# Two attention blocks mixed by a gate: the output projection is begun ahead of the second group of score products, which are issued inside it

## The chip, the cores and the metric

The kernel runs on one core of a Trainium2 chip. The metric is the device time of one execution in microseconds. PE is the matrix engine (PEld is its weight load), DVE the vector engine, ACT the scalar engine, POOL the GpSimd engine, SP the engine that issues most transfers.

## The reference

One input `x` (2048 x 512) goes through two attention blocks of 32 heads with 16 columns each, and a sigmoid gate mixes the results. Block A cuts the sequence into four segments, attends causally inside a segment and adds what a linear memory of the earlier segments gives. Block B is plain softmax attention over all 2048 positions.

```
g = sigmoid((x * gate_w).sum(-1))
# block A, segment s of 512 rows, per head
p = softmax(qs @ ks.T * 0.25 + causal mask)
o = sig(beta) * (phi(qs) @ M / (phi(qs) @ z)) + (1 - sig(beta)) * (p @ vs)
M, z = M + phi(ks).T @ vs, z + phi(ks).sum()
a = o_all @ A_wo
# block B, per head
b = softmax(q @ k.T * 0.25) @ v @ B_wo
out = g * a + (1 - g) * b
```

## The kernel before, in words

The first part projects `x` into q, k and v of both blocks, and the memory of block A is carried along. The order of the whole program is written out by hand; no planner reorders it. Only PSUM banks are picked while the program is being built, by rule: `bank(allowed)` takes the bank of the list that was used longest ago.

The second part is a loop `for k in range(32)`. Iteration `k` handles one unit of block A (four heads, one segment of 512 queries) and one of block B (four heads, the same 512 queries, all 2048 keys). It is cut into `NG` = 37 groups `n`: 32 of block B, 5 of block A. Each group does four things, and the rows of the profile carry their lines:

- `t_group` (L537): two score products with K, transposed (keys on partitions), `j` = 0 on rows 0 to 63 of the array and `j` = 1 on rows 64 to 127, each into a bank of its own out of the three banks `T3` = `tb0`, `tb1`, `mb`. Then two exponentials by ACT (L543) empty these banks into the tile `raw`.
- between the two products, one task of the row maxima for the next iteration, `s_b` (L474): two products on the two halves of the rows into one of two double banks, `sbk0` and `sbk1` (`rot("s", SBK)` alternates between them), and one DVE reduction over both (L476). In the text these are "the maxima products" and "the maxima reduction".
- `pv` (L559): four products of the exponentials of an earlier group with V into the bank `pvb`, on four column strips of the array.
- at set groups, side work. At group 0, the last `pv` of the previous unit of block A, and `fin_copy` (L566), a DVE copy of `pvb` to `pvs`.

From `k` = 9 to `k` = 30, group 1 also has `out_rows` (L644), one half of the output projection of a tile of 128 rows: twelve pairs of products on the two row halves, `j` = 0 into a bank from `misc()` (the oldest of `T3`), `j` = 1 into half of an `sbk`. Its left operands are `oh` and `ol`, the rounded part and the rest of the attention output, which `out_split` (L622 on ACT, L623 on POOL) makes at the end of each even iteration; the last four pairs use `ol`. After the third pair it runs the functions of its argument `inner`. The results leave by ACT (L652 or L658) and DVE (L653 or L659), in turn for `a` = 0 and `a` = 1. So the projection stands 22 times in the program, in eleven odd and eleven even iterations, the odd ones right behind an `out_split`.

Of the kernel before, what the change touches and what calls it, by code (L numbers as in the profile page):

```python
# [23 lines left out]
NT = SEQ // 128  # L24
# [10 lines left out]
def gated_mix_kernel(ctx, tc, xt, wq, wk, wv, wo, beta, wqkv, wob, gate_w, out):  # L35
# [49 lines left out]
    SBK = [PS.tile([128, 2, C], FT, name=f"sbk{i}") for i in range(2)]  # L85
    lru = []

    def bank(allowed):
        b = min(allowed, key=lambda a: max([n for n, x in enumerate(lru) if x is a], default=-1))
        lru[:] = [x for x in lru if x is not b] + [b]  # L90
        return b
# [3 lines left out]
    def misc():  # L95
        return bank(mode["misc"])
# [12 lines left out]
    def rot(key, lst):  # L109
        i = cnt.get(key, 0)  # L110
        cnt[key] = i + 1
        return lst[i % len(lst)]
# [287 lines left out]
    def q_of(u):  # L400
        return QA[u % 2] if u < 32 else QB[u % 3]

    def k_of(u, p):
        return KA[u % 2][:, p] if u < 32 else KB[(u - 32) % 3][:, p]

    def load_q(u):
        kd, qd, c = UN[u]
        load_qk(q_of(u), kd, 0, qd, c)

    def load_ka(u):  # L410
        kd, qd, c = UN[u]
        load_qk(KA[u % 2], kd, 1, qd, c)
# [105 lines left out]
    AT = {}  # L518
# [3 lines left out]
    def t_group(u, n, banks, between=()):  # L522


        kd, qd, c = UN[u]
        bs = [bank(banks) for _ in range(2)]
        c0 = 0
        for it, hs in (((n // 2, (n % 2 * 2, n % 2 * 2 + 1)),) if kd == "B" else GA[n]):
            q0 = 128 * it if kd == "A" else 0
            w = C - q0  # L530
            pn = it if kd == "B" else it % 2
            for j, h in enumerate(hs):
                if j:
                    for f in between:
                        f()
                r = slice(64 * j, 64 * j + 64)
                nc.tensor.matmul(bs[j][:, c0:c0 + w], k_of(u, h // 2)[r, 128 * it:128 * it + 128],  # L537
                                 q_of(u)[r, h // 2, q0:], start=True, stop=True)
                PT[u, it, h] = PTILE[pn % 2][:, 2 + j if (kd, it) == ("A", 2) else h][:, c0:c0 + w]
            c0 += w  # L540
        for j in range(2):
            pt = PTILE[pn % 2][:, 2 + j if (kd, n) == ("A", 4) else hs[j]]
            nc.scalar.activation(pt, bs[j], AF.Exp, scale=SCALE)  # L543
            if kd == "A":
                m = pt[:, :128] if n < 2 else pt.rearrange("p (a t) -> p a t", a=4)[:, ::3 if n < 4 else 2]
                nc.gpsimd.affine_select(out=m, in_=m, pattern=[[1, 128]] if n < 2 else [[0, 2], [1, 128]],  # L546
                                        compare_op=OP.is_ge, fill=0.0, base=0, channel_multiplier=-1)
# [89 lines left out]
            nc.sync.dma_start(outr[tt * 128:(tt + 1) * 128, :], AT["yo"])  # L637

    def out_rows(c, t, a, inner):
        b = [misc(), rot("s", SBK)[:, 0]]  # L640
        for n, (oi, wi, g) in enumerate([(oi, wi, g) for oi, wi in TERMS for g in range(4)]):
            for j in range(2):
                r = slice(64 * j, 64 * j + 64)
                nc.tensor.matmul(b[j], (AT["oh"], AT["ol"])[oi][r, g, a], (AT["wh"], AT["wl"])[wi][r, g, a],  # L644
                                 start=n == 0, stop=n == 11)
            if n == 2:
                for f in inner:
                    f()
                rot("s", SBK)
        if a == 0:  # L650
            AT["y"] = [AT["L"].tile([128, DM], FT, name=n) for n in ("yo", "yp")]
            nc.scalar.activation(AT["y"][0], b[0], AF.Copy)  # L652
            nc.vector.tensor_copy(AT["y"][1], b[1])  # L653
        else:
            tt = 4 * c + t
            y0, y1 = AT["y"]
            y2 = AT["L"].tile([128, DM], FT, name="yq")
            nc.scalar.activation(y2, b[0], AF.Copy)  # L658
            nc.vector.tensor_tensor(y1, b[1], y1, op=OP.add)  # L659
            nc.gpsimd.tensor_tensor(y0, y0, y2, op=OP.add)  # L660
            nc.gpsimd.tensor_tensor(y0, y0, y1, op=OP.add)
            nc.sync.dma_start(outr[tt * 128:(tt + 1) * 128, :], y0)
# [33 lines left out]
    def todo(fn, *a):  # L696
        return lambda: fn(*a)
# [90 lines left out]
    for blk in range(16):  # L788
# [9 lines left out]
        n = blk + 1 + (c == 2)  # L798
# [87 lines left out]
    T3 = TB + [MB]  # L886
# [4 lines left out]
    def pvs(k, n):  # L891

        ua, ub = k, 32 + k
        if n == 0:
            if k:
                pv(ua - 1, 2)
                fin_copy(ua - 1)
        elif k == 31 and n < 2 * NT:
            if n % 2 and n > 1:
                pv(ub, n // 2 - 1)  # L900
        elif 2 <= n < 2 * NT + 2:
            pv(ub, n // 2 - 1, n % 2 * 256, n % 2 * 256 + 256)
            if n == 2 * NT + 1:
                fin_copy(ub)
        elif n > 2 * NT + 1:
            m = n - 2 * NT - 2
            if m < 2:
                pv(ua, 0, 256 * m, 256 * m + 256)
            else:
                pv(ua, 1)  # L910
                pv(ua, 3)

    def extras(k):

        pre, post = {}, {}
        if not k:
            for n in range(4):
                pre[2 * n] = [fill[n - 4]]
        post[2 * S_LAST + 4] = [todo(m_rows, k + 1)]
        for n, at in [(k - 9, 1)] + [(23, 2 * OMI)] * (k == 31):  # L920
            if n >= 0:
                rows = (n // 8, n // 2 % 4, n % 2)
                pre[at] = [todo(out_rows, *rows, plan.pop((k, at))) if k < 31 else todo(out_mm, *rows)]
        return pre, post

    def beside(k, it):

        for f, it0, u in ((fin_load, NT + 1, 32 + k), (fin_rec, 5, 31 + k), (fin_bc, 6, 31 + k),
                          (fin_load, 1, k - 1), (fin_rec, 6, k - 1), (fin_bc, S_LAST + 2, k - 1)):
            if it == it0 and (k or it0 > NT):  # L930
                f(u)
        c, j = divmod(k - 1, 8)
        if k and j % 2:
            for kd, it0 in (("B", 9), ("A", 13)):
                if it == it0:
                    fin_norm(kd, j // 2, c)
        if k >= 8 and k % 2 == 0 and it == NT + 2:
            out_split(k // 8 - 1, k // 2 % 4)
        if (k, it) == (31, 4):
            grest = AT["grest"] = AT["o"][0][64:, 0, 0]  # L940
            nc.sync.dma_start(grest, GD[3 * C:].rearrange("(o t) -> o t", o=1).to_broadcast([64, C]))
        if (k, it) == (31, 9):
            grest = AT["grest"]
            nc.vector.tensor_scalar(grest, grest, nh[64:, 3:4], None, op0=OP.mult)
        if (k, it) == (31, NT + 2):
            fin_rec(63)
        if k == 31 and it == 13:
            o = AT["o"][1][:64, 3, 0]
            nc.gpsimd.tensor_tensor(o, o, AT["d"][0][:64], op=OP.mult)
        if k == 31 and it < 8 and it % 2 == 0:  # L950
            for a in range(2):
                tail_split(it // 2, slice(0, 3), a)


    plan = {}
# [14 lines left out]
    ex = [extras(k) for k in range(32)]  # L970
    for k in range(32):
        ua, ub = k, 32 + k
        banks = T3 + [b[:, 0] for b in SBK] * (k == 31)
        for n in range(NG):
            it = n // 2 if n < NG - 1 else NT + 2
            mid = plan.pop((k, n)) if n < 2 * NT and (k, n) in plan else []
            t_group(*(ub, n) if n < 2 * NT else (ua, n - 2 * NT), banks, mid)
            for f in plan.get((k, n), []) + ex[k][0].get(n, []):
                f()
            pvs(k, n)  # L980
            for f in ex[k][1].get(n, []):
                f()
            if n % 2 == 0 and n < NG - 1:
                continue
            beside(k, it)
            if it == S_LAST:
                m_chain(k + 1)
            if it == 4 and not k:
                late()
            if it == 4 and not k:  # L990
                load_q(ub + 2)
                for c in range(NC4):
                    load_kb(2, c)
            if it == NT and k < 29:
                load_q(ub + 3)
                load_kb(k + 3)
            if it == 6 and k < 31:
                load_q(ua + 1)
                load_ka(ua + 1)
                if (ua + 1) % 2 == 0:  # L1000
                    load_va(ua + 1)
            if it == 9:
                if k % 2 == 0 and k < 30:
                    load_vb(k // 2 + 1)
                if 1 <= k <= 4:
                    load_wo(k - 1)
# [55 lines left out]
```

## Time and profile before

| | |
|---|---|
| time, median of 3 runs | 1941.73 us (1938.82 to 1942.05) |
| profiled execution | 1942.89 us |
| its span in the trace | 1941.2 us |
| mean granted PE clock | 0.998 |
| busy share of the span | PE 99%, DVE 84%, ACT 74%, POOL 18% |
| first `out_rows` at | 787.71 us |

The profiled execution has its own time; the trace's span is 1.7 us shorter. The times within the trace are counted from the span's start. A busy PE counts a product from its start until a modelled end, so short stalls of PE are better read from start to start, or from the idle time of PEld.

### The profile page before, as it was taken

What the parts mean: (1) busy time and instruction counts of PE and PEld (TensorE: products, weight loads), DVE (VectorE), ACT (ScalarE), POOL (GpSimd) and SP (SyncE); (2) the same over time, 40 slices, a digit from 0 to 9 for tenths busy, and PEclk for the clock granted to TensorE, in tenths of its full rate; (3) what the DMA queues carried; (4) which work ended last, traced back from release to release, by engine and by line L of the source; (5) the groups of instructions that cost most, each with busy time, mean ns of one, the idle gap of its engine ahead of it and who ended that gap; (6) DMA issues with size and microseconds to landing.
All of it is one profiled execution on the core that took longest, in us unless ns stands there. A gap on an engine that the chain in (4) does not pass through costs nothing.

```text
span 1941.2 us, 44264 instructions
## 1 busy us (share of the span) xinstructions
PE 1915.3 (99%) x17749; PEld 933.8 (48%) x17749; DVE 1622.4 (84%) x1689; ACT 1438.0 (74%) x2710; POOL 345.1 (18%) x687
## 2 busy tenths in 40 slices
PE   7999998999999999999999999999999999999999
PEld 5887776444444444444444444444444444444445
DVE  6135765799999999999999999999999999999942
ACT  4233332688888888888888888888888888888894
POOL 5200000011211111112121212121212121212122
PEclk9999999999999999999999999999999999999999
DMA  7666556655543444444434344444444444434111
GB/s 218 167 208 189 183 186 180 162 118 115 100 116 88 106 90 105 88 115 86 115 88 115 88 115 88 109 95 109 95 101 99 95 104 92 107 90 107 50 49 59
DMA packets 163794, 222.54 MB, mean 115 GB/s; under 512 B 39916, under 2 KB 90556, under 8 KB 157828
## 3 DMA queue, kind: packets, MB, share of 16 engines
q1 hardware_dynamic: 159284, 211.41, 44.0%
q0 software_dynamic: 3248, 8.03, 2.2%
q8 instruction: 140, 2.29, 0.5%
q14 instruction: 66, 0.54, 0.1%
q10 hardware_dynamic: 1056, 0.26, 0.1%
HBM read 147.95 MB, written 68.16 MB: 111 GB/s over the span
## 4 chain that ended last, share of the span: by engine, by line
PE 95%; DVE 2%; DMA 1%; SPq 1%; ACT 0%; issue 0%; DVEq 0%; ACTq 0%
PE pvb L559 34%; PE tb L537 18%; PE sbk L474 12%; PE mb L537 9%; PE tb L304 4%; PE sbk L452 3%; PE tb L644 2%; PE mb L304 2%; PE sbk L287 1%; PE tb L287 1%; PE sbk L456 1%; PE mb L644 1%; PE pvb L304 1%; PE mb L287 1%; PE pvb L287 1%; DMA dA<-st 1%
## 5 line engine op out<-in xcount | busy, mean ns | idle before, releaser
L476 DVE TENSOR_REDUCE mxb<-sbk 128x2 f32<-128x1024 f32 x1024 | 1228.7, 1221 | 52.1 <-PE tb L537 24.0
L543 ACT ACTIVATE raw<-tb 128x512 f32<-128x512 f32 x1555 | 887.1, 598 | 125.7 <-PE tb L537 82.2
L559 PE MATMUL pvb<-raw,vb 128*17 128x256 f32 (+1 forms) x8072 | 639.8, 388 | 0.0
L543 ACT ACTIVATE raw<-mb 128x512 f32<-128x512 f32 x782 | 467.8, 598 | 60.3 <-PE mb L537 34.0
L474 PE MATMUL sbk<-xh,qb 64*128 64x512 f32 x1344 | 473.3, 442 | 4.8 <-DMA xh<-dB 3.4
L537 PE MATMUL tb<-qb,xh 64*128 64x512 f32 x872 | 351.2, 444 | 0.0
L559 PEld LDWEIGHTS pvb<-raw,vb 128*17 128x17 f32 x8072 | 134.9, 95 | 338.8 <-issue 333.4
L474 PE MATMUL sbk<-kb,qb 64*128 64x512 f32 x704 | 239.0, 442 | 0.0
L537 PEld LDWEIGHTS tb<-qb,xh 64*128 64x128 f32 x872 | 146.0, 184 | 174.4 <-issue 86.6
L537 PE MATMUL mb<-qb,xh 64*128 64x512 f32 x445 | 198.1, 445 | 0.0
L474 PEld LDWEIGHTS sbk<-xh,qb 64*128 64x128 f32 x1344 | 191.9, 184 | 11.6 <-DVE mxb L476 5.6
L537 PE MATMUL tb<-qb,kb 64*128 64x512 f32 x470 | 189.9, 444 | 0.8 <-DVE st L314 0.8
L546 POOL TENSOR_SCALAR_AFFINE_SELECT raw<-raw 128x256 f32<-128x256 f32 (+1 forms) x320 | 115.5, 361 | 354.2 <-ACT raw L543 346.3
L460 DVE TENSOR_REDUCE mx<-sbk 128x2 f32<-128x768 f32 (+1 forms) x128 | 136.7, 1090 | 23.2 <-POOL o L608 13.7
L537 PEld LDWEIGHTS mb<-qb,xh 64*128 64x128 f32 x445 | 82.0, 184 | 92.7 <-issue 47.9
L537 PEld LDWEIGHTS tb<-qb,kb 64*128 64x128 f32 x470 | 79.7, 184 | 96.1 <-issue 49.8
L537 PE MATMUL mb<-qb,kb 64*128 64x512 f32 x234 | 104.8, 448 | 0.0
L474 PEld LDWEIGHTS sbk<-kb,qb 64*128 64x128 f32 x704 | 96.7, 184 | 5.8 <-issue 3.2
L559 PE MATMUL pvb<-raw,va 128*17 128x256 f32 (+2 forms) x1280 | 94.8, 384 | 0.8 <-ACT pvs L568 0.8
L452 PE MATMUL sbk<-ka,qa 64*128 64x256 f32 (+3 forms) x512 | 87.8, 358 | 1.1
L311 ACT ACTIVATE st<-tb 128x512 fp32r<-128x512 f32 x33 | 19.8, 599 | 81.9 <-DVE phi L310 46.2
L603 POOL TENSOR_TENSOR o<-o,d 128x512 f32<-128x512 f32 x31 | 39.7, 1281 | 227.2 <-DMA d<-rd 177.1
(315 smaller groups left out, 2036.6 us busy)
## 6 DMA issues: line engine op xcount, KB each, us to landing
xh<-dB SPq DMA_DIRECT2D x38, 512.0 KB
vb<-vdB SPq DMA_DIRECT2D x16, 1088.0 KB
dB<-st SPq DMA_DIRECT2D x64, 256.0 KB
dA<-st SPq DMA_DIRECT2D x64, 256.0 KB
pd<-pvs SPq DMA_DIRECT2D x64, 256.0 KB
kb<-dB SPq DMA_DIRECT2D x22, 512.0 KB
xh<-dB SPq DMA_DIRECT2D x38, 256.0 KB
qb<-dB SPq DMA_DIRECT2D x64, 128.0 KB
```

Of the source, the lines that this page charges most:

```text
L287: nc.tensor.matmul(b, lhs, WV[wi][:, k, :], start=n == 0, stop=n == 11)
L304: nc.tensor.matmul(b, WS[ws][w][wi][:, k, :], (XH, XL)[xi][c][:, k, :], start=n == 0, stop=n == 11)
L452: nc.tensor.matmul(b[:, j, c0:c0 + n], q_of(u)[r, p, i * 128:(i + 1) * 128], k_of(u, p)[r, :n], start=True, stop=False)
L460: nc.vector.tensor_reduce(m[:, :, p, i], b[:, :, :n], axis=AX.X, op=OP.max)
L474: nc.tensor.matmul(b[:, j], q_of(u)[r, p, i * 128:(i + 1) * 128], k_of(u, p)[r, kc * C:(kc + 1) * C], start=True, stop=True)
L476: nc.vector.tensor_reduce(MXB[u][:, :, p, i, kc], b, axis=AX.X, op=OP.max)
L537: nc.tensor.matmul(bs[j][:, c0:c0 + w], k_of(u, h // 2)[r, 128 * it:128 * it + 128], q_of(u)[r, h // 2, q0:], start=True, stop=True)
L543: nc.scalar.activation(pt, bs[j], AF.Exp, scale=SCALE)
L546: nc.gpsimd.affine_select(out=m, in_=m, pattern=[[1, 128]] if n < 2 else [[0, 2], [1, 128]], compare_op=OP.is_ge, fill=0.0, base=0, channe ...
L559: nc.tensor.matmul(PVB[32 * h:32 * h + E + 1, q0 + lo:q0 + hi], vt[:, it, 4 * q + h, :], pt[:, lo:hi], start=it == 0 and lo == 0, stop=it ...
L603: nc.gpsimd.tensor_tensor(o, o, d, op=OP.mult)
L644: nc.tensor.matmul(b[j], (AT["oh"], AT["ol"])[oi][r, g, a], (AT["wh"], AT["wl"])[wi][r, g, a], start=n == 0, stop=n == 11)
```

## The change

In iterations 9 to 30 group 1 no longer issues its two score products before the projection. `out_rows` starts first, and after its third pair it calls `t_group` for group 1, which has the maxima task between its two products as every other group has. The bank that `out_rows` took is remembered as `AT["ob"]`, and group 2 picks its banks among the two others.

```
     def out_rows(c, t, a, inner):
-        b = [misc(), rot("s", SBK)[:, 0]]
+        AT["ob"] = misc()
+        b = [AT["ob"], rot("s", SBK)[:, 0]]
...
-                pre[at] = [todo(out_rows, *rows, plan.pop((k, at))) if k < 31 else todo(out_mm, *rows)]
+                pre[at] = [todo(out_rows, *rows, [todo(t_group, 32 + k, at, T3, plan.pop((k, at)))]) if k < 31 else
+                           todo(out_mm, *rows)]
...
     for k in range(32):
         ua, ub = k, 32 + k
-        banks = T3 + [b[:, 0] for b in SBK] * (k == 31)
         for n in range(NG):
+            banks = T3 + [b[:, 0] for b in SBK] * (k == 31)
             it = n // 2 if n < NG - 1 else NT + 2
             mid = plan.pop((k, n)) if n < 2 * NT and (k, n) in plan else []
-            t_group(*(ub, n) if n < 2 * NT else (ua, n - 2 * NT), banks, mid)
+            if 9 <= k < 31 and n == 2:
+                banks = [b for b in T3 if b is not AT["ob"]]
+            if not (9 <= k < 31 and n == 1):
+                t_group(*(ub, n) if n < 2 * NT else (ua, n - 2 * NT), banks, mid)
```

The order of PE's instructions at groups 0 and 1 of iteration 9. Before (L559 is the `pv` of group 0, L537 the score products, L644 the projection, L474 the maxima products; in brackets, on whom a product waits):

```order
L537 MATMUL mb_113<-qb2_70,kb0_89 128x512 [waits DMAHW2_49,DMAHW1_49]
L474 MATMUL sbk0_114<-xh0_87,qb0_68 128x512 [waits DVE_49]
...
L537 MATMUL tb1_111<-qb2_70,kb0_89 128x512 [waits Activation_49]
L559 MATMUL pvb_112<-raw8_86,va0_76 17x256 [waits Pool_49] x2
...
L537 MATMUL tb0_110<-qb2_70,kb0_89 128x512
L537 MATMUL mb_113<-qb2_70,kb0_89 128x512 [waits Activation_49]
L644 MATMUL tb1_111<-wh_2776,oh_2780 128x512 [waits Activation_49]
L644 MATMUL sbk1_115<-wh_2776,oh_2780 128x512 [waits DVE_49]
...
L474 MATMUL sbk0_114<-xh0_87,qb0_68 128x512 [waits DVE_49]
```

The same place in the changed kernel, where the projection's line is L645:

```order
L559 MATMUL pvb_112<-raw8_86,va0_76 17x256 [waits Pool_49] x2
...
L645 MATMUL tb0_110<-wh_2776,oh_2780 128x512 [waits Activation_49]
L645 MATMUL sbk1_115<-wh_2776,oh_2780 128x512 [waits DVE_49]
...
L537 MATMUL mb_113<-qb2_70,kb0_89 128x512 [waits Activation_49]
L474 MATMUL sbk0_114<-xh0_87,qb0_68 128x512 [waits DVE_49]
L474 MATMUL sbk0_114<-xh0_87,qb0_68 128x512
L537 MATMUL tb1_111<-qb2_70,kb0_89 128x512 [waits Activation_49]
```

Group 1's two score products moved behind the projection's third pair, around the maxima products. The projection now takes `tb0`, and group 1 takes `mb` and `tb1`, the two banks of group 0.

ACT at the same place, before (L652 empties the projection's bank):

```order
L543 ACTIVATE raw8_86<-mb_113 128x512 [waits PE_49]
L543 ACTIVATE raw8_86<-tb1_111 128x512 [waits PE_49]
L543 ACTIVATE raw8_86<-tb0_110 128x512 [waits PE_49,Pool_49]
L543 ACTIVATE raw8_86<-mb_113 128x512 [waits PE_49,Pool_49]
L652 ACTIVATE yo_7440<-tb1_111 128x512 [waits PE_49]
```

and in the changed kernel:

```order
L543 ACTIVATE raw8_86<-mb_113 128x512 [waits PE_49]
L543 ACTIVATE raw8_86<-tb1_111 128x512 [waits PE_49]
L543 ACTIVATE raw8_86<-mb_113 128x512 [waits PE_49,Pool_49]
L543 ACTIVATE raw8_86<-tb1_111 128x512 [waits PE_49,Pool_49]
L653 ACTIVATE yo_7440<-tb0_110 128x512 [waits PE_49]
```

ACT's order of work is the same; only the banks differ. DVE, POOL and SP keep their order.

## The prediction, written before the changed kernel was run

> **What bounds the kernel now.** I read the page first: the share of each engine and the chain of work that ended last.
>
> ```profile
> PE 1915.3 (99%) x17749; PEld 933.8 (48%) x17749; DVE 1622.4 (84%) x1689; ACT 1438.0 (74%) x2710; POOL 345.1 (18%) x687
> PE 95%; DVE 2%; DMA 1%; SPq 1%; ACT 0%; issue 0%; DVEq 0%; ACTq 0%
> ```
>
> PE carries 95% of the chain. So a moved instruction counts only where it changes when PE is held, or how its products follow each other. The second view is the one on the projection's line, L644, which says what its engine was idle for just before it:
>
> ```profile
> its engine sat idle before it (us, times) until:
>   ACT raw L543: 6.2, 22
> ```
>
> Each of the 22 projections begins with PE held by an exponential: 6.2 / 22 = 0.28 us each. That is 0.3% of the span and the whole field of this change. The third view is the timeline, around an odd iteration (k = 9) and an even one (k = 10); the columns are start, duration, engine, line, what it does and, in brackets, idle time and what ended it.
>
> ```profile
> 785.62 1.06 ACT L622 ACTIVATE oh<-o 128x1024 fp32r<-128x1024 f32 x1
> 786.57 0.60 ACT L543 ACTIVATE raw<-mb 128x512 f32<-128x512 f32 x1
> 786.59 1.23 DVE L476 TENSOR_REDUCE mxb<-sbk 128x2 f32<-128x1024 f32 x1 [0.94 <-PE tb L537]
> 786.77 2.39 POOL L623 TENSOR_TENSOR ol<-o,oh 128x1024 fp32r<-128x1024 f32 x1 [0.56 <-ACT oh L622]
> 787.04 0.50 PE L537 MATMUL tb<-qb,kb 64*128 64x512 f32 x1
> 787.05 1.19 ACT L543 ACTIVATE raw<-tb 128x512 f32<-128x512 f32 x2
> 787.22 0.50 PE L537 MATMUL mb<-qb,kb 64*128 64x512 f32 x1
> 787.71 0.18 PEld L644 LDWEIGHTS tb<-wh,oh 64*128 64x128 f32 x1 [0.31 <-ACT raw L543]
> 787.71 0.49 PE L644 MATMUL tb<-wh,oh 64*128 64x512 f32 x1
> 787.73 0.68 DVE L566 COPY pvs<-pvb 128x512 f32<-128x512 f32 x1
> 788.05 0.39 PE L644 MATMUL tb<-wh,oh 64*128 64x512 f32 x1
> 788.28 0.39 PE L644 MATMUL tb<-wh,oh 64*128 64x512 f32 x1
> 788.28 0.19 PEld L474 LDWEIGHTS sbk<-xh,qb 64*128 64x128 f32 x2
> 788.51 0.40 PE L474 MATMUL sbk<-xh,qb 64*128 64x512 f32 x2
> 790.81 0.40 PE L537 MATMUL tb<-qb,kb 64*128 64x512 f32 x1
> ...
> 835.79 1.09 ACT L543 ACTIVATE raw<-tb 128x512 f32<-128x512 f32 x2 [0.62 <-PE tb L537]
> 836.03 1.23 DVE L476 TENSOR_REDUCE mxb<-sbk 128x2 f32<-128x1024 f32 x1 [0.94 <-PE tb L537]
> 836.48 0.49 PE L537 MATMUL mb<-qb,xh 64*128 64x512 f32 x1
> 836.93 0.18 PEld L644 LDWEIGHTS tb<-wh,oh 64*128 64x128 f32 x1 [0.26 <-ACT raw L543]
> 837.27 0.39 PE L644 MATMUL tb<-wh,oh 64*128 64x512 f32 x1
> 840.05 0.40 PE L537 MATMUL mb<-qb,xh 64*128 64x512 f32 x1
> ```
>
> Read k = 9 from 787.04, where group 1 starts. Its two products take two banks, the projection needs the third, and that one still holds the second product of group 0, whose exponential runs 0.6 us after the first one's start at 787.05, to 787.65. The projection starts at 787.71. In k = 9 group 1's second product is late too (787.22 instead of beside 787.04): its bank is emptied at 786.57 + 0.60 = 787.17, because `oh` stood ahead of the exponentials on ACT. In k = 10 there is no `oh`, and only the projection is held, from 836.71 (one pair behind 836.48) to 836.93. These two idle times, 0.31 and 0.26, average to the 0.28 of the 22, so I take them for the eleven odd and eleven even iterations.
>
> **What the change removes.** The projection now takes the bank of the last group of the previous iteration, emptied by exponentials that stand on ACT ahead of `oh` (over at 786.68) in k = 9 and ahead of 835.79 in k = 10, so it can start where group 1 started. Pairs follow each other at (790.81 - 788.05) / 12 = 0.230 us in k = 9 and (840.05 - 837.27) / 12 = 0.232 in k = 10; the first pair after a stop takes 0.34 (787.71 to 788.05). There are 14 pairs from group 1 to group 2 in both orders: twelve of the projection, one of scores, one of maxima (in the new order a score product beside each maxima product). Without any wait group 2 would start 0.34 + 13 x 0.230 = 3.33 us behind group 1's old place; it was 790.81 - 787.04 = 3.77, so 0.44 is won. In k = 10: 840.05 - 836.48 = 3.57, against 0.34 + 13 x 0.232 = 3.35, so 0.22. The sum is 11 x 0.44 + 11 x 0.22 = 7.3 us.
>
> **What it adds.** Everything behind is now nearer to its inputs, and one input is too late. The maxima products of group 1 write the same `sbk0` as those of group 0, and need its reduction to be over. In k = 9 that ends at 786.59 + 1.23 = 787.82, in k = 10 at 836.03 + 1.23 = 837.26: both 0.78 behind group 1's old start. Before, these products came at 788.51, 0.7 behind it. Now they follow the third pair of the projection, at 0.34 + 2 x 0.23 = 0.80, and their weights would be loaded one pair earlier, at 0.57 (as at 788.28 for 788.51). What such a hold costs is seen in k = 8, which has no projection and where these products come early:
>
> ```profile
> 739.36 1.23 DVE L476 TENSOR_REDUCE mxb<-sbk 128x2 f32<-128x1024 f32 x1 [0.94 <-PE tb L537]
> 740.50 0.68 DVE L566 COPY pvs<-pvb 128x512 f32<-128x512 f32 x1
> 740.64 0.19 PEld L474 LDWEIGHTS sbk<-kb,qb 64*128 64x128 f32 x2 [0.20 <-DVE mxb L476]
> 740.64 0.50 PE L474 MATMUL sbk<-kb,qb 64*128 64x512 f32 x2
> 742.37 0.19 PEld L474 LDWEIGHTS sbk<-kb,qb 64*128 64x128 f32 x2
> 742.37 0.50 PE L474 MATMUL sbk<-kb,qb 64*128 64x512 f32 x2
> 742.71 0.38 PE L537 MATMUL tb<-qb,xh 64*128 64x512 f32 x1
> ```
>
> The reduction ends at 740.59, load and product both start at 740.64: 0.05 of signal, no wait for the copy on DVE, and then a product of 0.50 instead of 0.39, since its weights were not loaded ahead. So the held product really begins 0.78 + 0.05 + 0.11 = 0.94 behind group 1's old start instead of 0.80: 0.14 us later. What is queued behind it on PE: the other maxima product, which sits on the rows of the score product before it and isn't due before 1.03, so it loses nothing; and the second score product and all projection products of rows 64 to 127, which share its rows and follow at 0.23 each. That half runs 0.14 late until group 2's `pv`, which waits for both halves. Cost: 22 x 0.14 = 3.1 us. Nearest bounds: nothing, if the load gets through in time; 0.28, if the wait counts twice, once here and once where the halves meet again at `pv` (0.28 x 22 = 6.2).
>
> **What stays covered.** `oh` ends at 786.68, 0.36 before the projection's new start in k = 9; its slack was 1.03. `ol` ends at 789.16, 2.12 behind group 1's old start; its first pair is now the eleventh, at 0.34 + 9 x 0.23 = 2.41, so 0.29 is left (it would begin to cost if POOL took 2.7 instead of 2.39). The banks of group 1 are emptied 0.13 and 0.61 behind the old start, before 0.80 and 1.03. Its exponentials start about 0.7 later than before, and ACT was idle until L652 anyway; they end near 2.4, before group 2 at 3.3 wants the banks. Group 1's reduction still waits for the copy (to 788.41) and then ends near 789.8, while group 2's maxima products come near 790.5. From group 2 on, all waits stand to each other as before.
>
> **The sum.** -7.3 + 3.1 = -4.2 us: the profiled execution from 1942.89 to 1938.7, its span from 1941.2 to 1937.0. The median of the runs shown is 1941.73, 1.2 below the profiled execution; the same difference gives 1937.5. The measurement can tell about 0.2% from no change, 3.9 us here, so the forecast lies just beyond that bound.
>
> **A page against the row.** After the wait the first product takes 0.50 instead of 0.39, and the next pair follows at 0.34 instead of 0.23: a load that starts late is paid in full. The Trainium skill, TensorE: Matmul & The Clock Gate, in the section on the array as 16 blocks of 32x32, says that a product can begin before its weight load completes. By that rule the late load would cost nothing, which is the first rival below; the trace of k = 8 does not agree.
>
> **The rivals.**
>
> *The hold costs no more than the wait itself, or isn't there.* If the late load is free, 0.03 is lost per iteration: -7.3 + 22 x 0.03 = -6.6, 1935.1; if the reduction is in time, -7.3, 1934.4. For it: the reduction misses by 0.03 us only. Against it: the load wants the bank 0.23 earlier, and the 0.50 above. 0.18.
>
> *The gain is given back.* DVE is the next bound. Behind group 2 its five reductions stand without a gap:
>
> ```profile
> 791.65 5.93 DVE L476 TENSOR_REDUCE mxb<-sbk 128x2 f32<-128x1024 f32 x5
> 791.94 0.50 PE L537 MATMUL tb<-qb,kb 64*128 64x512 f32 x1
> 793.15 0.49 PE L537 MATMUL mb<-qb,kb 64*128 64x512 f32 x1
> ```
>
> They start (5.93 - 1.23) / 4 = 1.18 us apart, and a group takes PE 1.21 (791.94 to 793.15, scores to scores), so DVE makes up a lag by 0.03 per group only. If DVE comes out of the shorter projection with more lag, PE waits for it later: between 0 and -1.1 (the doubled hold), 1941.7 to 1940.6. Against it: DVE's reading of the projection (L653) sets this lag, and it moves together with group 2. 0.15.
>
> *Slower: the two halves out of step.* The trace shows the projection only with both halves starting within 0.02 us. After the hold they run 0.14 apart for some eleven pairs. If weights are then loaded less well ahead, a pair can cost 0.34 instead of 0.23, as behind the hold in k = 8 (742.37 to 742.71). From 4.2 / 22 / 11 = 0.017 us per pair on, the gain is gone; four pairs of eleven at 0.34 make 22 x 4 x 0.11 = 9.7, so +5.5 and 1947.2. Against it: each half then still has 0.23 for a load of 0.18. 0.07.
>
> That the change doesn't do what it says is ruled out by the order of instructions.
>
> **How the numbers follow.** The forecast has 0.60, with a hold of 0.10 to 0.20 (1936.6 to 1938.8); as its middle lies just past the bound of 0.2%, I put 0.33 of it on faster and 0.27 on no difference. The first rival adds 0.18 to faster, the second 0.15 to no difference, the third 0.07 to slower: 0.51, 0.42, 0.07. The range leaves out the third and the edge of the second: from 1934.3, just under no hold at all, to 1941.2.
>
> **What would show it.** Right: the idle time of 6.2 before the projection's line gone, its first product where group 1's stood, a new wait of L474 for L476 22 times, and group 2 about 3.47 us behind the projection's start in odd iterations and 3.49 in even ones. Wrong: pairs over 0.24 us behind the hold, a wait for `ol`, or waits for DVE behind group 2. Slower than 1941.7 would mean that the out-of-step halves or DVE cost over 0.33 us per iteration.

## The result: slower by 0.64%, against the forecast

| | before | changed |
|---|---|---|
| median | 1940.78 us (1938.82 to 1943.11, 6 runs) | 1953.05 us (1949.84 to 1958.31, 6 runs) |
| ratio | | 1.0064, 95% interval 1.0046 to 1.0082 |
| profiled execution, its span | 1942.89, 1941.2 | 1952.93, 1951.2 |

The forecast was 1937.5 us, with a range up to 1941.2. The measured time is 12 us above the end of the range, and none of the rivals describes where these went.

The profile after, first around the projection of iteration 9 (rows of the timeline, with others left out; L645 is the projection's line now):

```profile
782.14 1.23 DVE L476 TENSOR_REDUCE mxb<-sbk 128x2 f32<-128x1024 f32 x1 [0.95 <-PE tb L537]
782.32 2.40 POOL L623 TENSOR_TENSOR ol<-o,oh 128x1024 fp32r<-128x1024 f32 x1 [0.56 <-ACT oh L622]
782.59 0.49 PE L645 MATMUL tb<-wh,oh 64*128 64x512 f32 x1
783.16 0.18 PEld L537 LDWEIGHTS mb<-qb,kb 64*128 64x128 f32 x1
783.39 0.39 PE L537 MATMUL mb<-qb,kb 64*128 64x512 f32 x1
783.42 0.19 PEld L474 LDWEIGHTS sbk<-xh,qb 64*128 64x128 f32 x2
783.42 0.59 PE L474 MATMUL sbk<-xh,qb 64*128 64x512 f32 x2
783.85 0.39 PE L645 MATMUL tb<-wh,oh 64*128 64x512 f32 x1
783.99 0.39 PE L645 MATMUL sbk<-wh,oh 64*128 64x512 f32 x1
784.78 0.18 PEld L645 LDWEIGHTS tb<-wh,ol 64*128 64x128 f32 x1
785.01 0.39 PE L645 MATMUL tb<-wh,ol 64*128 64x512 f32 x1
785.92 0.40 PE L537 MATMUL mb<-qb,kb 64*128 64x512 f32 x1
786.08 0.47 PE L474 MATMUL sbk<-xh,qb 64*128 64x512 f32 x2
786.63 0.63 PE L559 MATMUL pvb<-raw,vb 128*17 128x256 f32 x8
```

Here it goes as the prediction had it. The projection starts at once, at 782.59. The maxima products are held: the reduction ends at 782.14 + 1.23 = 783.37, their load starts 0.05 later at 783.42, 0.83 behind the projection's start. The two row halves then stand 0.14 apart (783.85 and 783.99, still 785.92 and 786.08 at group 2, which is 3.33 and 3.49 behind the projection's start). `ol` is ready at 784.72, before its first weight load at 784.78 and its first product at 785.01. From group 1's old place to group 2's `pv` it is 786.63 - 782.59 = 4.04 us; before it was 791.38 - 787.04 = 4.34, with the row

```profile
791.38 0.63 PE L559 MATMUL pvb<-raw,vb 128*17 128x256 f32 x8
```

Now where the span grew. The start of iteration 30, before and after, in their timelines:

```profile
1823.17 0.50 PE L537 MATMUL tb<-qb,kb 64*128 64x512 f32 x1
```

```profile
1815.73 0.50 PE L645 MATMUL tb<-wh,oh 64*128 64x512 f32 x1
```

Up to there the changed kernel is ahead by 7.4 us, of which 787.04 - 782.59 = 4.45 is ahead of the first changed instruction and no effect of the change (the unchanged part took 781.4 to 787.4 us in the traces below). From there to the end it takes 1951.2 - 1815.7 = 135.5 us instead of 118.0: 17.5 us lost in the last two iterations, where the projection's place is the smaller part. The view on the score products' line, L537, in the last iteration, before:

```profile
L537 PE MATMUL sbk<-qb,xh x27: 385/494/501, 1870.1 to 1905.2; 64*128 64x512 f32 x27
L537 PE MATMUL tb<-qb,xh x25: 385/494/500, 1871.1 to 1905.2; 64*128 64x512 f32 x25
L537 PE MATMUL mb<-qb,xh x12: 385/493/500, 1876.3 to 1904.9; 64*128 64x512 f32 x12
  issue: 13.2, 20
  ACT raw L543: 4.3, 13
```

and after:

```profile
L537 PE MATMUL sbk<-qb,xh x64: 491/498/502, 1862.6 to 1914.4; 64*128 64x512 f32 x64
  ACT raw L543: 44.3, 68
```

Before, the 64 score products of block B went into five banks, in 35.1 us, and the idle times of PE and of PEld that ended with an exponential add up to 4.3 us. After, all 64 go into the two `sbk` banks, in 51.8 us, and these idle times add up to 44.3. They are no measure of the loss: both engines are counted, and the 0.85 us for which PEld is idle between two pairs of groups stand in both traces (ahead of 1886.40 and of 1892.02 below), before mostly under `issue`. The reason is in the diff: the line `banks = T3 + [b[:, 0] for b in SBK] * (k == 31)` moved into the loop over `n`. `bank` keeps its book by identity (`x is a`), and `b[:, 0]` makes a new object each time. Built once per iteration, the two objects age in the book like the other banks. Built in every group, they have never been used by the book, so they are always the two oldest. Five banks became two.

The timeline of the last iteration, after and before, shows how this costs time:

```profile
1886.40 0.18 PEld L537 LDWEIGHTS sbk<-qb,xh 64*128 64x128 f32 x2 [0.85 <-ACT raw L543]
1886.40 0.50 PE L537 MATMUL sbk<-qb,xh 64*128 64x512 f32 x2
1886.93 2.27 ACT L543 ACTIVATE raw<-sbk 128x512 f32<-128x512 f32 x4 [0.81 <-PE sbk L537]
1887.58 0.98 PE L537 MATMUL sbk<-qb,xh 64*128 64x512 f32 x2 [0.68 <-ACT raw L543]
1888.50 1.05 PE L559 MATMUL pvb<-raw,vb 128*17 128x512 f32 x8
1889.48 0.50 PE L537 MATMUL sbk<-qb,xh 64*128 64x512 f32 x2
```

```profile
1892.02 0.18 PEld L537 LDWEIGHTS sbk<-qb,xh 64*128 64x128 f32 x1 [0.85 <-issue]
1892.02 0.49 PE L537 MATMUL sbk<-qb,xh 64*128 64x512 f32 x1
1892.53 0.50 PE L537 MATMUL mb<-qb,xh 64*128 64x512 f32 x1
1893.98 0.49 PE L537 MATMUL sbk<-qb,xh 64*128 64x512 f32 x2
```

With two banks a product must wait for the exponential two products before it. The second group starts 1887.58 - 1886.40 = 1.18 us behind the first, where before all four products had started within 0.51 (1892.02 to 1892.53), and ACT then waits for PE (0.81). Two groups take 1889.48 - 1886.40 = 3.08 us instead of 1.96. Sixteen such pairs make 16 x 1.12 = 17.9, near the 17.5 lost.

### The profile page after: what moved, and what is told of

It is laid out like the page before. It is cut to its first block, busy times and chain, and to the rows that moved or that the text cites. A ratio compares the mean times of both kernels' runs of the same rounds, so it can differ in the third digit from the quotient of the medians.

```text
span 1951.2 us, 44246 instructions
## 1 busy us (share of the span) xinstructions
PE 1918.9 (98%) x17749; PEld 942.1 (48%) x17749; DVE 1624.5 (83%) x1689; ACT 1443.1 (74%) x2710; POOL 344.7 (18%) x687
## 4 chain that ended last, share of the span: by engine, by line
PE 96%; DVE 2%; ACT 1%; issue 1%; DMA 0%; SPq 0%; POOL 0%; DVEq 0%; ACTq 0%
PE pvb L559 33%; PE tb L537 17%; PE sbk L474 12%; PE mb L537 9%; PE tb L304 4%; PE sbk L452 3%; PE mb L304 2%; PE sbk L287 1%; PE tb L287 1%; PE sbk L645 1%; PE tb L645 1%; PE pvb L304 1%; PE sbk L537 1%; PE sbk L456 1%; PE mb L287 1%; PE pvb L287 1%
## 5 line engine op out<-in xcount | busy, mean ns | idle before, releaser
L543 ACT ACTIVATE raw<-tb 128x512 f32<-128x512 f32 x1525 | 869.0, 596 | 135.5 <-PE tb L537 94.3
L559 PE MATMUL pvb<-raw,vb 128*17 128x256 f32 (+1 forms) x8072 | 638.8, 388 | 0.0
L543 ACT ACTIVATE raw<-mb 128x512 f32<-128x512 f32 x769 | 458.2, 596 | 66.4 <-PE mb L537 40.8
L474 PE MATMUL sbk<-xh,qb 64*128 64x512 f32 x1344 | 474.6, 444 | 3.6 <-DMA xh<-dB 2.7
L537 PE MATMUL tb<-qb,xh 64*128 64x512 f32 x861 | 347.5, 441 | 0.0
L559 PEld LDWEIGHTS pvb<-raw,vb 128*17 128x17 f32 x8072 | 134.2, 95 | 341.3 <-issue 336.0
L474 PE MATMUL sbk<-kb,qb 64*128 64x512 f32 x704 | 239.4, 443 | 0.0
L537 PEld LDWEIGHTS tb<-qb,xh 64*128 64x128 f32 x861 | 145.1, 184 | 165.4 <-issue 82.1
L474 PEld LDWEIGHTS sbk<-xh,qb 64*128 64x128 f32 x1344 | 190.7, 185 | 9.5 <-DVE mxb L476 4.4
L537 PE MATMUL tb<-qb,kb 64*128 64x512 f32 x454 | 185.7, 444 | 0.8 <-DVE st L314 0.8
L537 PE MATMUL mb<-qb,xh 64*128 64x512 f32 x419 | 186.3, 445 | 0.0
L537 PEld LDWEIGHTS tb<-qb,kb 64*128 64x128 f32 x454 | 76.7, 184 | 92.2 <-ACT raw L543 44.6
L537 PEld LDWEIGHTS mb<-qb,xh 64*128 64x128 f32 x419 | 77.3, 184 | 85.7 <-ACT raw L543 42.4
L537 PE MATMUL mb<-qb,kb 64*128 64x512 f32 x250 | 110.6, 442 | 0.0
L474 PEld LDWEIGHTS sbk<-kb,qb 64*128 64x128 f32 x704 | 96.1, 184 | 5.7 <-issue 3.4
L559 PE MATMUL pvb<-raw,va 128*17 128x256 f32 (+2 forms) x1280 | 94.6, 384 | 0.3 <-ACT pvs L568 0.2
```

What stands on the lines that cost most here:

```text
L474: nc.tensor.matmul(b[:, j], q_of(u)[r, p, i * 128:(i + 1) * 128], k_of(u, p)[r, kc * C:(kc + 1) * C], start=True, stop=True)
L559: nc.tensor.matmul(PVB[32 * h:32 * h + E + 1, q0 + lo:q0 + hi], vt[:, it, 4 * q + h, :], pt[:, lo:hi], start=it == 0 and lo == 0, stop=it ...
```

## The experiments

Four kernels separate the two parts of the change and test the hold that the prediction charged.

**The changed kernel with the list built once.**

```
+        allowed = T3 + [b[:, 0] for b in SBK] * (k == 31)
         for n in range(NG):
-            banks = T3 + [b[:, 0] for b in SBK] * (k == 31)
+            banks = allowed
```

> The changed kernel, with the list of banks built once per iteration again, so that the last iteration (k = 31) rotates over five banks as before. Theory A (the last iteration lost its rotation: the two halves of the double banks are new objects in every group, were never used by the rule's book, and are picked every time): the stretch behind the last copy made by DVE shrinks from 87.4 to about 70 us, the idle time of 44.3 us before the score products of the last iteration goes to about 4, and the time is 3.2 to 4.2 us under the kernel before (ratio 0.9978 to 0.9984). Theory B (the reordering itself is what costs, for instance because the banks enter the last iteration in another order of age): the time stays about 12 us above the kernel before (ratio 1.006). Theory C (both): in between, above 1.000.

Measured: 1936.69 us against 1940.49, ratio 0.9978 (0.9969 to 0.9987). The last iteration is back at its old pace:

```profile
  ACT raw L543: 4.3, 13
```

Theory A holds: without the moved line the reordering is a gain of 0.22% (0.13% to 0.31%), and the prediction's sum said the same of it (4.2 of 1941.7 us).

**The moved line alone, in the kernel before.**

```
-        banks = T3 + [b[:, 0] for b in SBK] * (k == 31)
         for n in range(NG):
+            banks = T3 + [b[:, 0] for b in SBK] * (k == 31)
```

> The kernel before, with one line moved and nothing else: the list of banks is built anew in every group. The order of the projection is as before. Theory A: only the last iteration changes, its stretch grows from 70 to about 87 us, and the time is about 17 us above the kernel before (ratio 1.009). Theory B: no change (ratio 1.000). Theory C: in between.

Measured: 1955.6 us, ratio 1.0083 (1.0068 to 1.0098). The row of the score products in the last iteration:

```profile
L537 PE MATMUL sbk<-qb,xh x64: 491/498/502, 1865.4 to 1917.2; 64*128 64x512 f32 x64
```

It is the same 51.8 us as in the changed kernel. So the whole loss comes with this one line, and 0.9978 x 1.0083 = 1.0061 is the 1.0064 of both together.

**Group 1 behind the fourth pair, and behind the second.** Both with the list built once.

```
-            if n == 2:
+            if n == 3:
                 for f in inner:
```

> As e1_list_once, but group 1's score products and maxima task stand behind the fourth pair of the projection instead of the third. If the hold of 0.14 us per iteration comes from the maxima products being 0.03 us ahead of their bank, it goes: the products are due 1.03 us behind the projection's start and the bank is free at 0.83. Expected: another 3.1 us under e1_list_once, 6.3 to 7.3 us under the kernel before (ratio 0.9962 to 0.9967), both row halves starting together up to group 2. If the hold has another cause (the order of the products, the late halves), no difference from e1_list_once.

```
-            if n == 2:
+            if n == 1:
                 for f in inner:
```

> As e1_list_once, but behind the second pair. The bank of the maxima products is free at the same time, so they begin at 0.94 us behind the projection's start again, and are due at 0.57: a hold of 0.37 us instead of 0.14. Expected: 5 us above e1_list_once, about 1 us above the kernel before (ratio 1.0005 to 1.001). If a hold is mostly hidden behind the other row half, about as e1_list_once.

Measured: 1933.76 us behind the fourth pair, ratio 0.9974 (0.9964 to 0.9985), and 1941.05 us behind the second, 1.0006 (0.9997 to 1.0015). The timeline behind the fourth pair, around the projection's start:

```profile
783.68 1.23 DVE L476 TENSOR_REDUCE mxb<-sbk 128x2 f32<-128x1024 f32 x1 [0.95 <-PE tb L537]
784.13 0.49 PE L645 MATMUL tb<-wh,oh 64*128 64x512 f32 x1
784.97 0.39 PEld L474 LDWEIGHTS sbk<-xh,qb 64*128 64x128 f32 x2
785.18 0.60 PE L474 MATMUL sbk<-xh,qb 64*128 64x512 f32 x2
785.63 0.39 PE L645 MATMUL tb<-wl,oh 64*128 64x512 f32 x1
785.65 0.39 PE L645 MATMUL sbk<-wl,oh 64*128 64x512 f32 x1
788.06 0.61 PE L559 MATMUL pvb<-raw,vb 128*17 128x256 f32 x6
```

The load starts 0.84 behind the projection's start, but the product isn't due before 1.05; the halves stay together (785.63, 785.65), and the stretch is 788.06 - 784.13 = 3.93. Behind the second pair:

```profile
780.97 1.23 DVE L476 TENSOR_REDUCE mxb<-sbk 128x2 f32<-128x1024 f32 x1 [0.95 <-PE tb L537]
781.41 0.49 PE L645 MATMUL tb<-wh,oh 64*128 64x512 f32 x1
781.98 0.39 PE L537 MATMUL mb<-qb,kb 64*128 64x512 f32 x1
782.24 0.19 PEld L474 LDWEIGHTS sbk<-xh,qb 64*128 64x128 f32 x2 [0.31 <-DVE mxb L476]
782.25 0.50 PE L474 MATMUL sbk<-xh,qb 64*128 64x512 f32 x2
782.58 0.39 PE L537 MATMUL tb<-qb,kb 64*128 64x512 f32 x1
785.68 0.41 PE L559 MATMUL pvb<-raw,vb 128*17 128x256 f32 x4
```

The load starts at 0.83 again, the product was due at 0.57, and the stretch is 785.68 - 781.41 = 4.27. The same stretch, as a mean over the eleven odd and eleven even iterations of each trace, beside the 20 iterations from 9 to 29 and the last stretch, from the last copy of `pvb` by DVE to the end:

| us | odd | even | 9 to 29 | last stretch |
|---|---|---|---|---|
| before | 4.34 | 4.12 | 986.7 | 69.9 |
| line moved alone | 4.34 | 4.12 | 987.5 | 87.4 |
| changed kernel | 4.03 | 4.03 | 983.9 | 87.4 |
| list once, third pair | 4.03 | 4.03 | 984.1 | 70.0 |
| list once, fourth pair | 3.91 | 3.90 | 981.0 | 70.0 |
| list once, second pair | 4.26 | 4.25 | 988.2 | 69.9 |

The hold is real and has the size that was charged: 4.03 - 3.90 = 0.13 behind the third pair (forecast 0.14), 0.35 behind the second (forecast 0.37), none behind the fourth. The whole times don't settle how much the fourth pair brings over the third. By the medians it is 2.9 us, near the 3.1 expected, and 6.7 us under the kernel before. The ratio, which is not the quotient of the two medians (that is 0.9965), lies at 0.9974 above the 0.9962 to 0.9967 that was expected; its interval just reaches into that range and overlaps the one of the third pair. From iteration 9 to 29 the traces differ by 3.1 us, where 20 x 0.125 = 2.5 was due. This version beats the kernel before and the changed kernel.

**Two banks, or the wrong banks?** Two more kernels ask what of the last iteration's change costs: that there are only two banks, or that they are halves of the double ones.

```
-        banks = T3 + [b[:, 0] for b in SBK] * (k == 31)
+        banks = T3 if k < 31 else TB
```

> The kernel before, with the score products of the last iteration in two banks only, the single banks tb0 and tb1, instead of five. Theory A1 (two banks are too few, whichever they are: a product waits for the exponential two products before it): the stretch of the last iteration grows from 70 to about 87 us as with the list built in every group, and the time is about 15 us above the kernel before (ratio 1.008). Theory A2 (the halves of the double banks are what is slow, for instance because the tail of the output projection wants them too): no or little change (ratio under 1.003).

```
-        banks = T3 + [b[:, 0] for b in SBK] * (k == 31)
+        banks = T3
```

> The kernel before, with the score products of the last iteration in the same three banks as in all other iterations. Theory A1: as in the other iterations, where three banks are enough for a group of 1.2 us, a small loss at the most, 0 to 4 us (ratio 1.000 to 1.002), far from the 15 us of two banks. Theory A2: no change (ratio 1.000).

Measured, against 1939.86 us of the kernel before: 1956.35 us with two single banks, ratio 1.0078 (1.0061 to 1.0094); 1950.68 us with three, ratio 1.0051 (1.0036 to 1.0066). The idle time before the score products of the last iteration, with two and with three banks:

```profile
  ACT raw L543: 44.7, 69
```

```profile
  ACT raw L543: 31.0, 46
```

It is the number of banks: two single ones cost what the two halves cost (the last stretch is 87.5 us). The second expectation was wrong. I had taken three banks to be enough, as in the other iterations. There a group takes 1.2 us, with the maxima products in it; in the last iteration it takes 0.98 with five banks (1.96 / 2). With three, the fourth product of two groups waits for the first of their exponentials, and ACT for PE:

```profile
1896.11 0.49 PE L537 MATMUL mb<-qb,xh 64*128 64x512 f32 x1
1896.64 0.60 ACT L543 ACTIVATE raw<-mb 128x512 f32<-128x512 f32 x1 [0.53 <-PE tb L537]
1897.29 0.49 PE L537 MATMUL mb<-qb,xh 64*128 64x512 f32 x1 [0.45 <-ACT raw L543]
1898.70 0.50 PE L537 MATMUL tb<-qb,xh 64*128 64x512 f32 x2
```

The exponential ends at 1897.24, and the product into its bank starts at 1897.29. Two groups take 1898.70 - 1896.11 = 2.59 us, and 16 x (2.59 - 1.96) = 10.1 is near the 9.7 by which the last stretch grew (79.6 us).

## Why the prediction was wrong

The step that failed is the account of the change itself. The diff was read as a new order of the projection in iterations 9 to 30, and the moved line of the bank list as part of it, without a price. "From group 2 on, all waits stand to each other as before" was said of these iterations and silently of iteration 31. And the order of PE's instructions was read at groups 0 and 1 of iteration 9 only, so "That the change doesn't do what it says is ruled out by the order of instructions" didn't hold: in iteration 31 the order would have shown every score product writing an `sbk` bank. The missing term is +17.5 us; no bound and no rival had it, since all of them hung on the 22 projections. So the last sentence of the prediction, that a slower kernel would mean halves out of step or DVE, left out the cause that it had.

Point by point:

- *Held start of the projection, -7.3.* Right. Without the hold (fourth pair) the stretch is 0.43 shorter in odd and 0.21 in even iterations (before rounding), where 0.44 and 0.22 were worked out. From iteration 9 to 29 that makes 10 x 0.43 + 10 x 0.21 = 6.4 us, of which the trace gained 5.7; for the rest see the second rival.
- *The hold, +3.1.* Right in place, cause and size: 0.13 instead of 0.14. That a late load isn't free is shown by the second pair: the held product lasts 0.50, and its half is as late as the load plus 0.11. The prediction went too far the other way with "paid in full": 0.11 is less than the 0.19 that the load lasts. So what doesn't hold is "would cost nothing", and not the sentence it was drawn from, that a product can begin before its weight load completes (the Trainium skill, TensorE: Matmul & The Clock Gate, section on the array as 16 blocks of 32x32): here load and product are recorded as starting together, at 782.24 and 782.25.
- *What stays covered.* Right, but by less than was worked out. `ol` was ready 0.29 us ahead of its first product, as forecast (784.72 to 785.01); the weight load that needs it stands at 784.78, 0.06 behind it. The view on the projection's line no longer lists the exponentials. What it lists is 0.43 us at each start, the same behind an `oh` and without one, and about what group 1 showed at this place before (0.42):
```profile
  ACT oh L622: 4.7, 11
  issue: 4.7, 11
```

```profile
787.04 0.18 PEld L537 LDWEIGHTS tb<-qb,kb 64*128 64x128 f32 x1 [0.42 <-issue]
```

- *The sum of these, -4.2.* Right within the interval: 0.9978 is -4.3 us (-6.0 to -2.5). That it came so near is partly luck. Of the forecast, 10 x (0.44 - 0.14) + 10 x (0.22 - 0.14) = 3.8 lies between iterations 9 and 29, where the traces of the changed kernel and of its version with the list built once gained 2.8 and 2.6.
- *First rival, hold without a price.* Refuted by the 0.13.
- *Second rival, given back.* Partly seen. From 9 to 29 the changed kernel gained 2.8 us, where the shorter stretches make 10 x 0.31 + 10 x 0.09 = 4.0. The rest of an iteration grew by some 0.06 us, in steps of a few ns per group and in no wait that a view names. It may be scatter in part: of the traces with the unchanged order, the one with the line moved alone took 0.8 us longer than before over the same iterations. But those with two and with three banks in the last iteration took 986.8 and 986.7, as before, and all four traces with the new order gained 0.7 to 1.4 us less than their stretches say. The cause stays open.
- *Third rival, halves out of step.* Refuted as a loss: the halves ran 0.14 apart through the projection, and its pairs kept their pace (785.01 is five pairs behind 783.85: 0.232 each).
- *The new wait of L474 in the views of waits.* Not seen in that form: behind the third pair no idle time before L474 is listed in these iterations, though its load starts late (783.42): PEld is busy until 783.16 + 0.18 = 783.34, and none of these views lists an idle time as short as 0.08. Behind the second pair it is listed, 22 times:

```profile
  DVE mxb L476: 6.7, 22
```

## What to carry to other kernels

Read every line of a diff for every iteration that it runs in, and compare the order of instructions in the special iterations (first, last) too, not only where the change is meant to act: a line that was moved only so that a variable could be overwritten cost four times what the reordering won. A rule that picks the least recently used buffer must know a buffer by what it is, not by the object that names it. When an instruction is moved nearer to its input, compare the time at which its weight load wants that input with the time at which it comes, and move it by one slot more if it misses: here 0.03 us of lateness cost 0.13.

## What the runs showed of the hardware that was not expected

In these traces a held product waits at its weight load: behind the second and the third pair the load starts 0.05 us after the reduction's end (782.20 to 782.24, 783.37 to 783.42), and the product is recorded with it. Where the load starts behind the product's turn (second and third pair), the half runs late by the load's lateness against that turn plus 0.11 us. Where it starts 0.2 us ahead of the turn (fourth pair: 784.97 for 785.18), nothing is lost; what happens between these two no run shows. The hold behind the third pair has no row of idle time in the views; only the starts show it. And a row half of the array that runs behind the other neither caught up nor slowed the pairs: the gap is 0.14 us at 783.85 and 0.16 nine pairs later, at 785.92.
